# Cache loads issued as two halves, even and odd partitions, from two queues

## The chip, the cores and the metric

The kernel runs on one core of a Trainium2 chip. A core has five engines with instruction streams of their own: TensorE (PE), VectorE (DVE), ScalarE (ACT), GpSimd (POOL) and SyncE (SP). An engine takes its instructions in the order in which the program lists them for it; each may wait for counters (semaphores) that other engines or finished transfers advance. Data moves between the device's memory (HBM) and the on-chip buffer (SBUF, 128 partitions) by DMA. A DMA is issued by an engine as one of its instructions: the issuing engine waits for the semaphores that the transfer needs, hands the transfer to its own queue and goes on; the transfer's end advances another semaphore. SP's queue is called q1 in the profile, ScalarE's q10; the transfers of both run on the core's 16 DMA engines.

The metric is device time in microseconds (us) of one execution; several runs are given by their median. The profile comes from one further execution.

## The reference

Two layers of one decode step for two sequences (B = 2, one token each, width 576). A layer is attention over a cache of 8192 positions with 32 heads of 128, and a gated MLP of width 4608. All is float32, and both layers use the same weights and the same caches.

```python
def _A_ref(x, k_cache, v_cache, wq, wo):
    q = (x @ wq).reshape(B, Sq, H, Dh).transpose(0, 2, 1, 3)
    scores = jnp.einsum("bhqd,bhkd->bhqk", q, k_cache) * (Dh ** -0.5)
    p = _softmax(scores, axis=-1)
    o = jnp.einsum("bhqk,bhkd->bhqd", p, v_cache)
    return o.transpose(0, 2, 1, 3).reshape(B, Sq, H * Dh) @ wo
...
def _B_ref(x, w_gate, w_up, w_down):
    g = jnp.einsum("bsd,df->bsf", x, w_gate)
    u = jnp.einsum("bsd,df->bsf", x, w_up)
    return jnp.einsum("bsf,fd->bsd", _gelu(g) * u, w_down)
...
x = x + _A_ref(_layernorm(x), A_k_cache, A_v_cache, A_wq, A_wo)
x = x + _B_ref(_layernorm(x), B_w_gate, B_w_up, B_w_down)
x = x + _A_ref(_layernorm(x), A_k_cache, A_v_cache, A_wq, A_wo)
x = x + _B_ref(_layernorm(x), B_w_gate, B_w_up, B_w_down)
```

## The kernel before, in words

**Items.** The attention is cut into items: for each sequence 15 pairs of heads (`PAIRS` = 30 items of two heads) and four items of one head (`SINGLE`). The keys or values of a pair are 16384 rows of 128 floats; each partition holds 128 consecutive rows, 64 KB, in 8 parts of 16 rows (`PART`). `Item.source` lays the cache out in this way, partition first. Layer 0 takes the items in rising order, layer 1 in falling order; what layer 0 loads last (the keys of the last two items and the values of the last three, with pieces of others) stays on chip for layer 1 (`KEYS_HELD`, `VALUES_HELD`, `kept`).

**Space.** One tile, `space`, is nearly the whole SBUF: six slots of 32 KB per partition for the caches (a pair takes two), the last of which makes way to four smaller places in a ring for weights and odd pieces. The class `Arena` keeps account of it while the program is written.

**Loads.** `plan_first`, `plan_mlp` and `plan_second` put all loads of weights and caches into one list in the order in which they are wanted. `pump` takes from its head what finds free space, and is called after each `done(key)`, at the point of the program that last reads a piece of data. A load's DMA so stands in the program right behind the reader that frees its place, and waits for that reader's semaphore. All loads are issued by SP, which has nothing else to do. `cache`, `half`, `one` and `several_parts` (whole pairs or items, half items, single parts, several parts) all call `load`, whose DMA is line 168; weights have DMAs of their own (lines 233 to 322), and line 233 (`by_rows`) brings one item's keys by rows. ScalarE issues only the eight small loads of x (line 143) and half of the output (line 1201).

**The attention.** For an item VectorE multiplies the keys by the query (L743, from `multiply`), GpSimd folds the products in half (L772) and VectorE sums them (L775, from `add_up`, which then frees the keys). Maximum and softmax follow: L799, a transposition on PE (L801), L807, PE again (L809), then ScalarE's scaling of the maximum (L824) and its exponentials (L832). PE multiplies the weights by the values (L913, from `values`, which frees them); two of a pair's eight value parts go another way, VectorE L880, GpSimd L883, PE L891 (`weigh`, `folded`). L927, L928, L936 gather an item's context, and L943, L955, L957 divide it. `half_products` (L615) makes layer 1's queries from halves of wq.

At the start of layer 1 the first five items (`waited`) run in units of one part. There ScalarE copies the query to SBUF (L740), GpSimd multiplies the last four rows with it (L759), and ScalarE sums the last seven rows itself (L765):

```python
            if rows < every and k == 0:
                nc.scalar.copy(q, qb[n])
...
            for j in range(r, every):
                nc.scalar.activation(
                    u[:, j, :], u[:, j, :], AF.Copy, accum_out=S[n][:, base(n, k) + j:base(n, k) + j + 1]
                )
```

Near the end of layer 0 ScalarE copies one part of an item's keys to PSUM before VectorE overwrites it with products (L733). The order of the work on each engine is written out by hand in `attention`: in the loop over items the units of item n alternate with softmax, folding, values and context of the items before.

The functions that the diff touches, and those that call them, with the line numbers of the profile:

Of the kernel before, what the change touches and what calls it, by code (L numbers as in the profile page):

```python
# [24 lines left out]
JC = 16  # L25
# [37 lines left out]
ITEMS = [Item(b, h, 2) for h in range(0, H - 2, 2) for b in range(B)]  # L63
# [62 lines left out]
def decode_layers(ctx, tc, x_in, kc, vc, wq, wo, wg, wu, wd, out):  # L126
    nc = tc.nc
# [12 lines left out]
    for c in range(4):  # L140
        for s in range(2):
            lo = 32 * c + s * B
# [16 lines left out]
    def part_at(at, n):  # L159
        return space[:, at:at + n]  # L160
# [4 lines left out]
    def load(at, n, src, lo, hi):  # L165

        t = part_at(at, (hi - lo) * PART).rearrange("p (j d) -> p j d", d=DH)
        nc.sync.dma_start(t, ITEMS[n].source(src)[:, lo * JC:hi * JC, :])

    def cache(key, src, n, slots=None):  # L170

        parts = ITEMS[n].parts

        def make():
            at = arena.pair(key) if slots is None else arena.slots(key, slots, parts)
            if at is None:
                return False
            load(at[0], n, src, 0, parts)
            ready[key] = dict(enumerate(map(part, at)))
            places[key] = at  # L180
            return True

        queue.append(make)

    def half(key, src, n, k, slot):

        def make():
            at = arena.slots(key, (slot,), 4, k)
            if at is None:
                return False  # L190
            load(at[0], n, src, k, k + 4)
            ready.setdefault(key, {}).update((k + i, part(a)) for i, a in enumerate(at))
            return True

        queue.append(make)

    def one(key, src, n, k, where):

        def make():
            at = arena.ring((key, k), PART) if where is None else arena.take((key, k), places[where[0]][where[1]], PART)  # L200
            if at is None:
                return False
            load(at, n, src, k, k + 1)
            ready.setdefault(key, {})[k] = part(at)
            return True

        queue.append(make)
# [250 lines left out]
    for b in range(B):  # L458
        rows = ident.rearrange("p (c v i r) -> p i r v c", c=4, v=4, i=2)[:, :, :, b, :]
# [769 lines left out]
```

## Time and profile before

| | |
|---|---|
| three runs | 2681.36 us median, 2681.06 to 2681.51 |
| the profiled execution | 2681.31 us, of which the span of its instructions is 2679.5 us |
| mean granted TensorE clock | 0.627 |
| read from HBM | 1152.39 MB, 430 GB/s over the span |
| instructions in the span | 15405 |

The page gives the busy time of each engine over the span; PE is the matmuls, PEld the weight loads beside them. L743 is line 743 of the kernel, "x" a count of instructions. A queue's share is the time that its packets took on the 16 DMA engines. In the timeline a row is one instruction or several alike: start, length, engine, line, operation, what it writes and reads; in brackets the idle time of its engine before it and what ended that. SPq and ACTq rows are the sequencers', which issue DMAs; the length there is that of the issue and not of the transfer. The chain of waits follows the last instruction back through what released each step. For the DMA engines the page shows, in 40 slices of the span:

```profile
DMA  9999999999999999999999999999999999999998
GB/s 423 437 429 434 436 434 432 431 436 433 431 434 434 434 433 432 436 428 427 417 417 431 436 433 434 434 430 434 435 432 432 436 434 433 431 437 434 428 430 385
```

### The profile page before, as it was taken

How to read it: one execution, taken by the hardware profiler on the slowest of the kernel's cores; microseconds unless marked ns; L12 is line 12 of the kernel's file. 1: busy time of each engine (PE TensorE's matmuls, PEld its weight loads, DVE VectorE, ACT ScalarE, POOL GpSimd, SP SyncE). 2: the span in 40 equal slices, each digit the busy share in tenths (PEclk: the TensorE clock that was granted, in tenths of full speed). 3: DMA queues.
4: the chain of work that ended last, by engine and by line, in shares of the span. 5: the costliest groups of instructions: out<-in, count | busy, mean ns of one | idle time of the engine just before them, and what ended most of it. 6: DMA issues, size and time to landing. Idle time of an engine off the chain costs nothing.

```text
span 2679.5 us, 15405 instructions
## 1 busy us (share of the span) xinstructions
PE 880.8 (33%) x6198; PEld 268.7 (10%) x6198; DVE 1992.6 (74%) x907; ACT 165.7 (6%) x792; POOL 1560.5 (58%) x411
## 2 busy tenths in 40 slices
PE   1313332232223233334663323223222323332346
PEld 0000000000000000011221000000000000000022
DVE  4877888888788888867038778888888888888740
ACT  0000000000000000001026000000000000000000
POOL 2546676667667666744028457666766666676620
PEclk8666655665665566566986665566566556655678
DMA  9999999999999999999999999999999999999998
GB/s 423 437 429 434 436 434 432 431 436 433 431 434 434 434 433 432 436 428 427 417 417 431 436 433 434 434 430 434 435 432 432 436 434 433 431 437 434 428 430 385
DMA packets 29207, 1153.39 MB, mean 430 GB/s; under 512 B 3256, under 2 KB 3280, under 8 KB 4048
## 3 DMA queue, kind: packets, MB, share of 16 engines
q1 hardware_dynamic: 29096, 1152.40, 99.8%
q8 instruction: 48, 0.79, 0.1%
q14 instruction: 23, 0.19, 0.0%
q10 hardware_dynamic: 40, 0.01, 0.0%
HBM read 1152.39 MB, written 0.00 MB: 430 GB/s over the span
## 4 chain that ended last, share of the span: by engine, by line
DMA 67%; DVE 19%; PE 8%; POOL 2%; ACT 2%; issue 1%; another core or an unknown queue 0%; SPq 0%; POOLq 0%; ACTq 0%; DVEq 0%
DMA space<-in_A_k_cache_dram 59%; DVE space L743 17%; PE acc L891 3%; DMA space<-in_B_w_down_dram 2%; DMA space<-in_B_w_gate_dram 2%; POOL space L772 2%; DVE scores L775 2%; PE bank L658 1%; DMA space<-in_A_v_cache_dram 1%; DMA space<-in_B_w_up_dram 1%; PE bank L809 1%; ACT prz L832 1%; PE acc L913 1%; DMA space<-in_A_wo_dram 1%; PE bank L845 1%
## 5 line engine op out<-in xcount | busy, mean ns | idle before, releaser
L772 POOL TENSOR_TENSOR space<-space 128x3072 f32<-128x3072 f32 (+4 forms) x221 | 1128.4, 5106 | 459.1 <-DVE space L743 330.7
L743 DVE TENSOR_TENSOR space<-space,bank 128x6144 f32<-128x6144 f32 (+4 forms) x223 | 1111.9, 4987 | 344.7 <-DMA space<-in_A_k_cache_dram 273.7
L775 DVE TENSOR_REDUCE scores<-space 128x48 f32<-128x3072 f32 (+4 forms) x223 | 568.7, 2550 | 92.1 <-POOL space L772 92.1
L913 PE MATMUL acc<-space,prz 128*16 128x512 f32 (+1 forms) x3312 | 510.1, 780 | 357.9 <-DMA space<-in_A_v_cache_dram 346.4
L883 POOL TENSOR_TENSOR space<-space 128x2048 f32<-128x2048 f32 x147 | 398.0, 2708 | 392.3 <-DVE space L880 376.8
L658 PE MATMUL bank<-qsb,few 4*64 4x128 f32 (+1 forms) x256 | 46.1, 436 | 894.8 <-DVE space L743 887.1
L880 DVE TENSOR_TENSOR space<-space,bank 128x4096 f32<-128x4096 f32 x49 | 216.6, 4421 | 1.7
L913 PEld LDWEIGHTS acc<-space,prz 128*16 128x16 f32 (+1 forms) x3312 | 108.7, 117 | 742.0 <-issue 449.7
L824 ACT ACTIVATE nbs<-bank 128x2 f32<-128x2 f32 (+1 forms) x68 | 11.6, 171 | 2010.4 <-PE bank L809 1957.1
L658 PEld LDWEIGHTS bank<-qsb,few 4*64 4x64 f32 (+1 forms) x256 | 20.6, 201 | 914.2 <-DVE space L743 897.4
L580 POOL TENSOR_TENSOR rstd<-ve,few 128x1 f32<-128x1 f32 x4 | 2.2, 551 | 171.3 <-DVE ve L578 171.3
L891 PE MATMUL acc<-space,few 128*16 128x512 f32 x98 | 92.6, 1048 | 0.0
L801 PE MATMUL bank<-ident,m 128*1 128x128 f32 x68 | 20.7, 305 | 196.1 <-DVE m L799 195.9
L936 PE MATMUL bank<-few,wide 128*32 128x4 f32 (+1 forms) x272 | 20.9, 200 | 170.1 <-DVE wide L928 170.1
L1153 DVE STREAM_TRANSPOSE gu<-acc 128x288 f32<-128x288 f32 x4 | 1.9, 484 | 92.6 <-ACT acc L1151 92.6
L832 ACT ACTIVATE prz<-scores,nbs 64x128 f32<-64x128 f32 (+1 forms) x128 | 50.7, 396 | 11.7 <-POOL prz L822 8.9
L765 ACT ACTIVATE space<-space 128x128 f32<-128x128 f32 x164 | 48.4, 297 | 19.5 <-DVE space L743 16.5
L809 PE MATMUL bank<-m,few 1*128 1x2 f32 (+1 forms) x136 | 39.0, 353 | 28.1 <-DVE m L807 28.1
L584 DVE TENSOR_TENSOR x<-bank,x 128x144 f32<-128x144 f32 x4 | 1.2, 308 | 59.4 <-PE bank L1186 39.7
L927 DVE TENSOR_TENSOR acc<-acc,few 128x512 f32<-128x512 f32 x34 | 23.5, 691 | 29.2 <-PE acc L913 29.2
L936 PEld LDWEIGHTS bank<-few,wide 128*32 128x32 f32 x272 | 19.1, 154 | 216.0 <-issue 211.0
L955 ACT ACTIVATE oT<-bank,rinv 32x8 f32<-32x8 f32 x108 | 28.1, 260 | 190.1 <-PE bank L936 189.1
(105 smaller groups left out, 495.8 us busy)
## 6 DMA issues: line engine op xcount, KB each, us to landing
space<-in_A_v_cache_dram SPq DMA_DIRECT2D x7, 4096.0 KB
space<-in_A_k_cache_dram SPq DMA_DIRECT2D x6, 4096.0 KB
space<-in_B_w_gate_dram SPq DMA_DIRECT2D x9, 1152.0 KB
space<-in_B_w_up_dram SPq DMA_DIRECT2D x9, 1152.0 KB
space<-in_B_w_down_dram SPq DMA_DIRECT2D x8, 1152.0 KB
space<-in_A_wq_dram SPq DMA_DIRECT2D x9, 1024.0 KB
space<-in_A_wo_dram SPq DMA_DIRECT2D x2, 4608.0 KB
space<-in_A_k_cache_dram SPq DMA_DIRECT2D x4, 2048.0 KB
```

The costliest lines, as they stand in the source:

```text
L658: nc.tensor.matmul(qb[n][to, :], pick[32 * c:32 * c + 4, r:r + 1].to_broadcast([4, P // it.heads]), qsb[32 * c:32 * c + 4, (h % 4) * DH:(h ...
L743: nc.vector.tensor_tensor(out=u[:, :r, :], in0=t[:, :r, :], in1=qb[n].unsqueeze(1).to_broadcast([P, r, DH]), op=ALU.mult)
L765: nc.scalar.activation(u[:, j, :], u[:, j, :], AF.Copy, accum_out=S[n][:, base(n, k) + j:base(n, k) + j + 1])
L772: nc.gpsimd.tensor_tensor(out=half, in0=half, in1=u[:, :r, DH // 2:], op=ALU.add)
L775: nc.vector.tensor_reduce(out=S[n][:, base(n, k):base(n, k) + own_rows(n, k, m)], in_=prod.pop((n, k)), axis=AX.X, op=ALU.add)
L809: nc.tensor.matmul(mT[n][:, :heads], ones[0:1, :], m1[:, :heads], start=True, stop=True)
L832: nc.scalar.activation(pr[at, lo:].rearrange("p (g e) -> p g e", e=4)[:, 0:it.rows // 2 * it.heads:2 * it.heads, :], s[at, :it.rows].rearr ...
L880: nc.vector.tensor_tensor(out=t, in0=t, in1=share.unsqueeze(2).to_broadcast([P, rows, DH]), op=ALU.mult)
L883: nc.gpsimd.tensor_tensor(out=t[:, :rows - less], in0=t[:, :rows - less], in1=t[:, less:rows], op=ALU.add)
L891: nc.tensor.matmul(accumulator(n)[0:16, :], owner[:, 8 * ITEMS[n].b:8 * ITEMS[n].b + 16], part_at(arena.live[key, lo][0], 4 * DH), start=F ...
L913: nc.tensor.matmul(accumulator(n)[32 * c:32 * c + m, :], pr[:, at:at + m], t[g // 4][:, g % 4 * 4:g % 4 * 4 + 4, :].rearrange("p j d -> p ...
L936: nc.tensor.matmul(po[lo:lo + 32, i, :c], t[:, i::GH], of[:, :c], start=True, stop=True)
```

## The change

`load` issues two DMAs where it issued one. The destination and the source are cut by partition: the even partitions are issued by SP, the odd ones by ScalarE. Both halves have the rows of the whole load, 64 KB each for a pair, and 64 partitions. Each half is waited for by whoever reads the data. The point of the program at which they are issued is the same for both: ScalarE's half stands among ScalarE's own instructions there, and waits for the readers that free the place as SP's half does. Loads of weights, the eight loads of x and line 233 stay as they are.

```diff
@@ -165,7 +165,9 @@
     def load(at, n, src, lo, hi):
 
         t = part_at(at, (hi - lo) * PART).rearrange("p (j d) -> p j d", d=DH)
-        nc.sync.dma_start(t, ITEMS[n].source(src)[:, lo * JC:hi * JC, :])
+        rows = ITEMS[n].source(src)[:, lo * JC:hi * JC, :]
+        for engine, p in ((nc.sync, 0), (nc.scalar, 1)):
+            engine.dma_start(t[p::2], rows[p::2])
 
     def cache(key, src, n, slots=None):
```

## The prediction

> **What bounds the kernel now.** First the page: busy time per engine, the queues, the chain that ended last.
>
> ```profile
> PE 880.8 (33%) x6198; PEld 268.7 (10%) x6198; DVE 1992.6 (74%) x907; ACT 165.7 (6%) x792; POOL 1560.5 (58%) x411
> q1 hardware_dynamic: 29096, 1152.40, 99.8%
> DMA 67%; DVE 19%; PE 8%; POOL 2%; ACT 2%; issue 1%; another core or an unknown queue 0%; SPq 0%; POOLq 0%; ACTq 0%; DVEq 0%
> ```
>
> SP's queue (q1) alone keeps the 16 DMA engines 99.8% busy; two thirds of the chain is DMA. What is left to gain by keeping the engines fuller is 0.2% of 2679.5 us, 5.4 us. The view by stretches (the stretch and its length, busy time of PE, its weight loads, DVE, ACT and POOL with their instructions, the granted clock, the busy share of the DMA engines, GB/s) says at what rate they run:
>
> ```profile
> 2.00:26.00 24.00, 0.23 (x1) 0.23 (x2) 4.12 (x24) 0.00 (x0) 0.00 (x0) 1.00 0.97 417
> 26.00:82.00 56.00, 12.94 (x89) 3.51 (x89) 36.03 (x14) 2.90 (x7) 20.57 (x5) 0.64 0.99 431
> 300.00:700.00 400.00, 115.74 (x628) 31.85 (x628) 331.35 (x119) 17.90 (x75) 268.78 (x63) 0.59 1.00 433
> 1180.00:1240.00 60.00, 23.52 (x125) 8.41 (x125) 39.86 (x38) 6.35 (x21) 25.07 (x13) 0.66 1.00 432
> 1283.00:1359.00 76.00, 47.40 (x695) 19.66 (x684) 5.77 (x26) 1.42 (x4) 0.55 (x1) 0.98 1.01 418
> 1388.00:1464.00 76.00, 33.84 (x186) 10.45 (x181) 62.76 (x73) 53.37 (x336) 58.96 (x48) 0.67 1.01 426
> ```
>
> In steady attention it is 433 GB/s with a share of 1.00. One turn of that stage in the timeline:
>
> ```profile
> 568.44 6.55 DVE L743 TENSOR_TENSOR space<-space,bank 128x6144 f32<-128x6144 f32 x1 [3.43 <-DMA space<-in_A_k_cache_dram]
> 576.29 0.17 ACT L824 ACTIVATE nbs<-bank 128x2 f32<-128x2 f32 x1 [29.44 <-PE bank L809]
> 579.98 0.33 SPq L168 DMA_DIRECT2D space<-in_A_k_cache_dram  x1
> 607.14 6.55 DVE L743 TENSOR_TENSOR space<-space,bank 128x6144 f32<-128x6144 f32 x1 [4.70 <-DMA space<-in_A_k_cache_dram]
> ```
>
> DVE waits for keys, and the load issued at 579.98 is used at 607.14, 27.2 us later. Its 8.39 MB (two heads of 8192 x 128 floats) take 19.4 us at 433 GB/s, so some 7.8 us of transfers were still queued ahead. That queue is the cover: an issue may come 7.8 us late in this stage before an engine has nothing to move.
>
> **The change part by part.**
>
> *More and smaller transfers.* Line 168 issues this many loads:
>
> ```profile
> L168 SPq DMA_DIRECT2D space<-in_A_k_cache_dram x72: 327/328/424, 10.8 to 2512.6; - x72
> L168 SPq DMA_DIRECT2D space<-in_A_v_cache_dram x69: 327/328/431, 37.9 to 2545.8; - x69
> ```
>
> 141 more DMAs, the same bytes in the same rows. The nearest row is the stretch 1180 to 1240, whose loads are of 4 MB as most halves will be: 432 GB/s against 433 is 0.02 us for 4.19 MB, at most 141 x 0.02 = 3 us, and within rounding. The far bound is the stretch from 1283 with loads of 1152 KB: 1.18 MB at 418 takes 2.82 us, at 433 2.72, so 0.10 us each, 14 us in all; but its pieces are 9 KB and ours stay 8 to 64 KB. Below nothing is excluded but for the 5.4 us above. I take 1 us.
>
> *The rate with two queues at work.* No row shows half the partitions moving in each of two queues. Nearest is the start, where ScalarE's eight small loads of x run beside the bulk of SP's: 417 GB/s in 2 to 26 against 431 in 26 to 82, at worst 3.3%, with the start itself in it. The cache loads are 1152.4 MB less 101.4 MB of weights (shapes of the inputs, twice) and 2.4 MB of line 233, so 1048.6 MB, 2422 us at 433: the upper bound of this kind is 80 us, the lower 0. I take 0, since a packet of a given size has the same work in either queue and the engines were full.
>
> *Issuing from ScalarE, steady state.* An issue costs its sequencer 0.33 us, and what stands behind a waiting issue waits too. In program order the key load of 579.98 stands behind ScalarE's exponentials, which follow its L824 of 576.29, and ahead of the next L824, one turn (607.14 - 568.44 = 38.7 us) later; a value load stands between the same two. That next L824 needs the next item's maximum, which comes after what the loads wait for. So ScalarE, 6% busy, is there in time and holds nobody: 0 us, covered by an idle of 29.44 us in the row above.
>
> *The start.*
>
> ```profile
> 44.62 6.55 DVE L743 TENSOR_TENSOR space<-space,bank 128x6144 f32<-128x6144 f32 x1 [16.60 <-DMA space<-in_A_k_cache_dram]
> 73.04 0.33 SPq L168 DMA_DIRECT2D space<-in_A_k_cache_dram  x1
> ```
>
> Now wq (9.4 MB) goes first, then the first keys, used at 44.6. After the change the odd half of those keys goes beside wq, behind ScalarE's loads of x, and the odd half of the second keys beside their even half: the first keys are complete up to 4.19 MB later, 9.7 us. The next issue, now at 73.04, moves with it. Queued by then are 9.4 + 3 x 8.39 = 34.6 MB, 80 us at 433, done at about 82: a cover of 9 us. The term is 1 us (0 to 3).
>
> *End of layer 0.*
>
> ```profile
> 1218.78 1.86 ACT L733 COPY kept<-space 128x2048 f32<-128x2048 f32 x1
> 1222.09 2.28 DVE L743 TENSOR_TENSOR space<-space,bank 128x2048 f32<-128x2048 f32 x1
> 1227.54 0.33 SPq L168 DMA_DIRECT2D space<-in_A_v_cache_dram  x1
> 1228.52 2.29 DVE L743 TENSOR_TENSOR space<-space,bank 128x2048 f32<-128x2048 f32 x1 [3.03 <-DMA space<-in_A_k_cache_dram]
> 1269.19 3.60 PE L913 MATMUL acc<-space,prz 128*8 128x512 f32 x16 [1.50 <-DMA space<-in_A_v_cache_dram]
> 1279.58 1.90 PE L913 MATMUL acc<-space,prz 128*8 128x512 f32 x16 [3.10 <-DMA space<-in_A_v_cache_dram]
> ```
>
> The load of 1227.54 takes the slot that PE's values free. In the program it stands ahead of the copy to `kept` (L733), and the in-place product at 1222.09 may not start before that copy. So copy and product move to about 1227.9 and 1229.7, and the next item's product from 1228.52 to about 1233.1: 4.6 us late. PE's waits for data at 1269 and 1279, 1.50 + 3.10, take that up. 1 us (0 to 4).
>
> *Start of layer 1, the main term.* Here ScalarE sums rows itself (L765) and is 70% busy.
>
> ```profile
> 1380.97 0.54 SPq L268 DMA_DIRECT2D space<-in_A_wq_dram  x1
> 1382.31 0.27 ACT L740 COPY qs<-bank 128x128 f32<-128x128 f32 x1 [0.43 <-PE bank L658]
> 1382.61 1.75 DVE L743 TENSOR_TENSOR space<-space,bank 128x1536 f32<-128x1536 f32 x1 [12.26 <-ACT qs L740]
> 1388.40 0.33 SPq L168 DMA_DIRECT2D space<-in_A_k_cache_dram  x1
> 1389.78 1.04 PE L615 MATMUL acc<-space,xt 128*4 128x512 f32 x8 [0.60 <-DMA space<-in_A_wq_dram]
> 1390.84 0.41 ACT L730 COPY space<-prz 128x264 f32<-128x264 f32 x1 [0.98 <-PE acc L615]
> 1405.57 0.33 SPq L168 DMA_DIRECT2D space<-in_A_v_cache_dram  x1
> 1422.28 0.30 ACT L765 ACTIVATE space<-space 128x128 f32<-128x128 f32 x1
> 1424.79 0.33 SPq L168 DMA_DIRECT2D space<-in_A_k_cache_dram  x1
> 1424.61 1.75 DVE L743 TENSOR_TENSOR space<-space,bank 128x1536 f32<-128x1536 f32 x1 [2.06 <-ACT qs L740]
> 1436.19 0.31 ACT L765 ACTIVATE space<-space 128x128 f32<-128x128 f32 x1 [2.48 <-DVE space L743]
> 1438.53 1.75 DVE L743 TENSOR_TENSOR space<-space,bank 128x1536 f32<-128x1536 f32 x1 [1.71 <-ACT qs L740]
> 1439.77 0.33 SPq L168 DMA_DIRECT2D space<-in_A_k_cache_dram  x1
> ```
>
> The load of 1388.40 is recorded inside `half_products(0)`, where PE frees a quarter of wq, ahead of the loop over heads and so ahead of the first L740. On SP it waits alone. On ScalarE the copy L740 stands behind it, and behind that DVE's first product of the layer: both move from 1382.3 to 1388.8, 6.4 us. Of that 0.98 goes into the wait that ScalarE's L730 had for PE anyway; 5.4 us stays. Later two more loads wait where ScalarE works now: 1424.79 stands ahead of sums that began at 1422.28 (2.5 + 0.33 us), 1439.77 ahead of sums from 1436.19 (3.6 + 0.33). Behind both comes an L740 that DVE waits for. Some ten other issues add 0.33 each where ScalarE is busy, say 1 us of it on the path. So DVE is late by 6.4 us near 1421, 9.2 from 1425, 13 from 1440.
>
> The cover: the quarter of wq issued at 1380.97 is used at 1389.78, 8.8 us later, of which its 1.05 MB take 2.5 at 418; 6.3 us were ahead of it. From there to 1405.57 the plan issues 1024 + 2 x 1152 + 1024 + 2048 + 3 x 1024 KB = 9.70 MB, 22.8 us at 426, and 24.6 us go by: 4.5 us are left. To 1439.77 come 3072 + 2 x 2048 + 1024 + 2048 + 4096 KB, 34.5 us of work in 34.2 us: 4.8 us. After that come loads of 4 MB, 29.5 us of work in the 24 to the next turn: 10 us. The DMA engines lack work by the largest of lateness less cover: 6.4 - 4.5 = 2, 9.2 - 4.8 = 4.4, 13 - 10 = 3. With the time from an issue to its first byte, which no row shows apart, I take 5 us (0 with full absorption, 13 without cover). Time the engines stand idle is lost for good, as everything later is bound by them.
>
> **The sum** is made against the profiled execution, 2681.31 us (span 2679.5 and 1.8 around it); the median of the runs, 2681.36, is the same. 2681.3 + 1 + 0 + 0 + 1 + 1 + 5 = **2689 us**, +0.3%. About 0.2% (5.4 us) is what a measurement of this kernel can tell from no change; the line to slower is 2686.7.
>
> **The rivals.**
>
> *Nothing is lost (chance 0.22).* The even halves of SP alone keep the engines fed while ScalarE holds back the odd ones, and the 4.5 to 5 us of cover at the start of layer 1 are enough because DVE makes up its lateness in waits of its own. For it: share 1.01 throughout that stretch. Against it: DVE is 83% busy there (62.76 of 76). It decides if DVE's lateness at 1440 stays under 5 us. 2681.3 + 1 + 1 = 2683.
>
> *The halves move more slowly (0.16).* If 64 partitions are dealt out so that two DMA engines write to the same place while another place has none, a packet takes up to twice as long: 1048.6 MB at 216 instead of 433 is 2422 us more, about 5100; a mix in which one packet in thirty meets another costs the 80 us of the bound above, 2770. Against it: in 1283 to 1359 weights whose source has 64 rows run at 418, not at half. For it: none of these has 64 partitions at its destination. [...]
>
> *Gain (0.06).* Loads that no longer wait in one line fill the idle 0.2%: 2681.3 - 5 = 2676. Against it: the share of 1.00 at 433 in 400 us.
>
> *ScalarE's waits have no cover (0.08).* The lateness of 13 us at layer 1, 4 at the end of layer 0 and 3 at the start are paid in full: 2702.
>
> **How the numbers follow.** My forecast has 0.48; its own range is 2684 to 2697, about a sixth of it under 2686.7. Slower: 0.40 + 0.16 + 0.08 = 0.64; same: 0.08 + 0.22 = 0.30; faster 0.06. The range 2680 to 2760 takes in the forecast, nothing lost, the waits without cover and most of the 80 us bound of the rate; the doubled packets above it (0.12) and the gain (0.06) stay out.
>
> **What would show it.** q10 carries about 524 MB, q1 the rest, and steady stretches stay at 433 GB/s. The first L740 of layer 1 comes 6 us later against the load at its side, DVE's wait for it grows, and the DMA share dips between 1390 and 1445, some 5 us of idle in all. ScalarE's waits in steady state are unchanged. I am wrong if steady stretches run below 430 GB/s, if that dip is missing, or if ScalarE holds DVE in steady state.

## The result and the profile after

| | median, us | runs |
|---|---|---|
| before, beside it | 2681.44 | 2681.06 to 2682.32 |
| changed kernel | 2694.11 | 2693.40 to 2694.61 |

The ratio is 1.0046, with a 95% interval from 1.0034 to 1.0059: slower by 12.7 us. Ratios leave out runs more than 1.5% above the fastest of the same kernel, which only e7 below has (three of six). The profiled execution has a span of 2692.1 us, 12.6 more than before. In the changed kernel the line numbers are higher by 2 (L743 is now L745, L740 is L742, L765 is L767, L168 is L170).

The page, as before: busy time, the 40 slices of GB/s, the two queues, the chain of waits.

```profile
PE 878.6 (33%) x6198; PEld 270.6 (10%) x6198; DVE 1992.7 (74%) x907; ACT 165.3 (6%) x792; POOL 1561.1 (58%) x411
GB/s 405 435 436 432 429 435 432 436 434 432 434 433 432 432 434 433 435 428 427 417 391 401 435 435 432 433 433 435 433 435 433 432 432 434 433 435 432 433 429 382
q1 hardware_dynamic: 20072, 628.11, 54.4%
q10 hardware_dynamic: 11320, 524.31, 45.1%
DMA 66%; DVE 19%; PE 9%; POOL 3%; issue 1%; ACT 1%; ACTq 0%; DVEq 0%; another core or an unknown queue 0%; POOLq 0%; SPq 0%
```

The engines' busy times are those of before within 2.2 us. The bytes are split between two queues, and almost every slice has its old rate. Three slices don't: the first (405, was 423) and the 21st and 22nd (391 and 401, were 417 and 431), which are the start of the program and the start of layer 1. The view by stretches, with the same bounds as before (the last two columns are the busy share of the DMA engines and GB/s), says the same:

```profile
2.00:26.00 24.00, 0.40 (x2) 0.40 (x2) 4.13 (x24) 0.00 (x0) 0.00 (x0) 1.00 0.87 373
26.00:82.00 56.00, 12.51 (x83) 2.65 (x82) 33.70 (x12) 2.12 (x3) 18.44 (x4) 0.66 1.01 431
300.00:700.00 400.00, 116.16 (x628) 31.99 (x628) 330.57 (x118) 17.89 (x75) 269.01 (x64) 0.59 1.00 433
1180.00:1240.00 60.00, 22.67 (x145) 7.33 (x133) 34.34 (x28) 6.88 (x22) 21.94 (x11) 0.70 1.00 431
1388.00:1464.00 76.00, 34.88 (x182) 10.79 (x178) 52.25 (x64) 44.28 (x274) 48.22 (x40) 0.64 0.95 380
```

The loss stands in two rows: 373 for 417 GB/s in the first 26 us, 380 for 426 in 1388 to 1464. Since the same bytes are moved, it can be followed through the span: for each time t of before, take the bytes that the DMA engines had moved, and see how much later another kernel had moved as many. This table is worked out from the packets' records; e1 to e12 are the experiments below.

```
us later than before, when as many bytes had been moved
at us  after   e1    e2    e3    e4    e6    e8    e9    e12
   20   -0.1   0.0   0.0   0.0   0.0   0.0   0.0   0.0   0.0
   30    2.9   3.2   0.0   3.1   0.0   0.0   3.1   0.0   0.0
  100    2.9   3.1   0.2   3.1   2.5   0.0   3.1   0.5   0.0
 1000    3.0   3.2   0.1   3.3   2.7   0.0   3.3   0.8   0.1
 1380    2.7   3.2   0.2   3.0   2.7   0.0   3.0   1.1   0.0
 1400    6.9   3.1   3.8   3.1   6.3   3.1   3.0   1.0   3.1
 1420    9.5   3.0   6.3   3.3   8.9   4.8   3.4   1.1   4.3
 1440   11.0   3.3   7.2   3.3  10.4   5.1   3.3   1.0   4.6
 1460   11.6   3.1   7.8   3.7  11.2   5.7   3.1   1.1   5.5
 1540   12.0   3.0   7.7   4.1  11.9   5.6   3.1   1.2   5.4
 2500   12.1   3.1   7.8   4.2  11.9   5.7   3.4   1.3   5.4
```

The count is of all 16 DMA engines together. In the changed kernel 2.9 us are lost before 30 us, nothing from there to 1380, 9.3 between 1380 and 1540, and 0.1 from there to 2500. The other half microsecond of the 12.6 comes behind the last row.

**The first 3 us.** The timeline (start, length, engine, line) shows when the first cache loads are issued and first used; the last row is of the view of waits: SP's queue at line 170, what it waited for, us in all, times, the longest.

```profile
25.24 5.01 SPq L170 DMA_DIRECT2D space<-in_A_k_cache_dram  x2
25.19 5.10 ACTq L170 DMA_DIRECT2D space<-in_A_k_cache_dram  x2
47.63 6.55 DVE L745 TENSOR_TENSOR space<-space,bank 128x6144 f32<-128x6144 f32 x1 [19.79 <-DMA space<-in_A_k_cache_dram]
SPq L170 <- DMA space<-in_A_wq_dram: 17.3, 1, 17.3
```

Each of the first two rows is two issues: halves of the first keys at 25.2, halves of the second keys near 29.8. Before, SP issued the first keys at 10.80; now both of their halves are held until wq has landed, though wq and the first keys have different columns of `space` (from 31744 up, and below 16384, by the program's constants). By 25 us there is nothing else to move: the stretch 22 to 26 has a DMA share of 0.46, and had 1.08. (The view counts a packet where it starts, so a short stretch can show a little more than 1.)

**The start of layer 1.** These rows answer to those of 1382 to 1440 in the prediction.

```profile
1391.62 0.50 ACTq L170 DMA_DIRECT2D space<-in_A_k_cache_dram  x1
1392.16 0.27 ACT L742 COPY qs<-bank 128x128 f32<-128x128 f32 x1 [7.29 <-PE acc L617]
1392.46 1.75 DVE L745 TENSOR_TENSOR space<-space,bank 128x1536 f32<-128x1536 f32 x1 [19.27 <-ACT qs L742]
1433.49 0.50 ACTq L170 DMA_DIRECT2D space<-in_A_k_cache_dram  x1
1434.04 0.31 ACT L767 ACTIVATE space<-space 128x128 f32<-128x128 f32 x1 [2.87 <-PE acc L915]
1436.37 1.75 DVE L745 TENSOR_TENSOR space<-space,bank 128x1536 f32<-128x1536 f32 x1 [5.03 <-ACT qs L742]
1451.63 0.50 ACTq L170 DMA_DIRECT2D space<-in_A_k_cache_dram  x1
1454.57 1.75 DVE L745 TENSOR_TENSOR space<-space,bank 128x1536 f32<-128x1536 f32 x1 [6.00 <-ACT qs L742]
```

ScalarE's half stands ahead of its copy L742. ScalarE stands idle 7.29 us there, until PE (matmuls L617) has freed the place, issues at 1391.62, copies at 1392.16, and only then can DVE start the layer: at 1392.46, where 1382.61 + 3.0 was due, after a wait of 19.27 us (was 12.26). The two other loads that wait on ScalarE hold DVE in the same way, 5.03 us (was 2.06) and 6.00 (was 1.71).

### The profile page after: what moved, and what is told of

It is laid out like the page before. It is cut to its first block, busy times and chain, and to the rows that moved or that the text cites. A ratio compares the mean times of both kernels' runs of the same rounds, so it can differ in the third digit from the quotient of the medians.

```text
span 2692.1 us, 15866 instructions
## 1 busy us (share of the span) xinstructions
PE 878.6 (33%) x6198; PEld 270.6 (10%) x6198; DVE 1992.7 (74%) x907; ACT 165.3 (6%) x792; POOL 1561.1 (58%) x411
## 4 chain that ended last, share of the span: by engine, by line
DMA 66%; DVE 19%; PE 9%; POOL 3%; issue 1%; ACT 1%; ACTq 0%; DVEq 0%; another core or an unknown queue 0%; POOLq 0%; SPq 0%
DMA space<-in_A_k_cache_dram 57%; DVE space L745 17%; PE acc L893 3%; DMA space<-in_B_w_up_dram 3%; POOL space L774 2%; DVE scores L777 2%; DMA space<-in_A_wo_dram 2%; PE bank L660 1%; PE acc L915 1%; DMA space<-in_A_v_cache_dram 1%; DMA space<-in_A_wq_dram 1%; PE bank L811 1%; DMA space<-in_B_w_down_dram 1%; DMA space<-in_B_w_gate_dram 1%; ACT prz L834 1%
## 5 line engine op out<-in xcount | busy, mean ns | idle before, releaser
L745 DVE TENSOR_TENSOR space<-space,bank 128x6144 f32<-128x6144 f32 (+4 forms) x223 | 1111.9, 4987 | 359.7 <-DMA space<-in_A_k_cache_dram 270.3
L767 ACT ACTIVATE space<-space 128x128 f32<-128x128 f32 x164 | 48.3, 295 | 27.4 <-DVE space L745 13.2
L761 POOL TENSOR_TENSOR space<-space,qs 128x512 f32<-128x512 f32 x23 | 29.4, 1279 | 32.4 <-ACT qs L742 32.4
```

What stands on the lines that cost most here:

```text
L745: nc.vector.tensor_tensor(out=u[:, :r, :], in0=t[:, :r, :], in1=qb[n].unsqueeze(1).to_broadcast([P, r, DH]), op=ALU.mult)
L761: nc.gpsimd.tensor_tensor(out=u[:, rows:every, :], in0=t[:, rows:every, :], in1=q.unsqueeze(1).to_broadcast([P, every - rows, DH]), op=ALU ...
L767: nc.scalar.activation(u[:, j, :], u[:, j, :], AF.Copy, accum_out=S[n][:, base(n, k) + j:base(n, k) + j + 1])
```

## The experiments

The theory: 9 us come from ScalarE's in-order stream at the start of layer 1, 3 us from the first load's wait for wq. The rivals: halves cost something each, two queues cost something, the loss is spread over all issues. A counter of the calls of `load` picks loads: 0 is the first keys, 70 to 83 are the 14 loads issued from 1388 to 1450. Medians are beside those of before in the same group of runs, 2681.70 for e1 to e4, 2681.56 for e5 to e8, 2681.45 for e9 to e12.

### e1: both halves by SP

```diff
-        for engine, p in ((nc.sync, 0), (nc.scalar, 1)):
+        for engine, p in ((nc.sync, 0), (nc.sync, 1)):
```

> Both halves issued by SP, ScalarE issues none. Theory (ScalarE's in-order stream costs 9 us at the start of layer 1, the first load's wait for wq 3 us at the start): the 9 us go, the 3 us stay, 2684.4. Rival 'halves' (141 more DMAs, smaller ones, completion semaphores used again sooner): all 12 us stay, 2693 to 2694. Rival 'two queues' (the sharing of the DMA engines between two queues): both losses go, 2681.4.

2684.86 us, ratio 1.0011 (1.0003 to 1.0020). The 9 us are gone and 3 stay. The stretch at the start of layer 1 is whole again:

```profile
1388.00:1464.00 76.00, 35.94 (x197) 10.41 (x189) 62.83 (x73) 54.61 (x343) 58.62 (x48) 0.70 1.01 427
```

In the table e1 loses 3.2 us before 30 us and nothing after: 141 more DMAs, each of half the size, cost nothing that shows.

### e2 and e3: one part of the change alone

```diff
+        i = len(calls)
+        calls.append(i)
+        if not 70 <= i < 84:        # e3: if 70 <= i < 84:
+            nc.sync.dma_start(t, rows)
+            return
```

> Only the 14 loads at the start of layer 1 are halves by SP and ScalarE, the other 127 are whole on SP. Theory: 2681.4 + 9 = 2690.5, with the same waits of VectorE for ScalarE's copies as in the changed kernel. Rival 'spread out' (the loss is a little for each of 141 issues or DMAs): 12.7 x 14/141 = 1.3, so 2682.7.

> The reverse: those 14 loads are whole on SP, the other 127 are halves by SP and ScalarE. Theory: the 3 us of the start alone, 2684.4. Rival 'spread out': 12.7 x 127/141 = 11.4, so 2692.8.

e2 took 2690.60 us, ratio 1.0033 (1.0020 to 1.0045); e3 2685.87, 1.0014 (1.0005 to 1.0023). The 14 loads at the start of layer 1 bring 8.9 us, the other 127 bring 4.2, and 8.9 + 4.2 is within half a microsecond of the whole, 12.7. A loss spread over the issues would have put 1.3 on the one and 11.4 on the other. e3's column of the table has 3.1 us at the start and 0.8 more between 1440 and 1540, where the halves begin again.

### e8: only the three that wait ahead of ScalarE's copies are whole

```diff
+        if i in (70, 79, 81):
+            nc.sync.dma_start(t, rows)
+            return
```

> The three loads of the start of layer 1 that wait ahead of ScalarE's copies (1388.40, 1424.79 and 1439.77 us) are whole on SP, the other 138 are halves. Theory that these three waits are all of the 9 us: 2684.4, with what the other eleven issues cost by themselves on top (at most 11 x 0.5 us): up to 2686. Rival 'all fourteen share the loss': 9 x 11/14 = 7 stay, 2691.5.

2686.01 us, ratio 1.0016 (1.0008 to 1.0025). With three of 141 loads back on SP, the loss at the start of layer 1 is gone (table: 3.0 at 1380, 3.1 at 1460). The first row is of the timeline, the second of the stretches:

```profile
1385.60 1.75 DVE L751 TENSOR_TENSOR space<-space,bank 128x1536 f32<-128x1536 f32 x1 [12.27 <-ACT qs L748]
1388.00:1464.00 76.00, 34.83 (x196) 10.31 (x188) 62.80 (x73) 54.03 (x343) 58.70 (x48) 0.71 1.01 426
```

DVE's first product waits 12.27 us as before, and comes 3.0 us later than before, which is the loss at the start of the program. The eleven other issues on ScalarE, 0.5 us each, cost nothing there that the table shows. The median is 1.2 us above that of e1, in which ScalarE issues no cache load; the two intervals overlap, so whether ScalarE's other issues cost about a microsecond in all isn't settled.

### e6 and e12: one load alone, halved or whole on ScalarE

```diff
+        if i != 70:                 # e6: load 70 alone is halved
+            nc.sync.dma_start(t, rows)
+            return
...
+        (nc.scalar if i == 70 else nc.sync).dma_start(t, rows)      # e12: no halves
```

> One load alone is halved, the one of 1388.40 us at the start of layer 1, whose odd half stands on ScalarE ahead of the layer's first copy of the query. Theory: VectorE's first product waits about 6 us longer and the DMA engines lack work for all or most of it before 1420: 2681.4 + 4 to 6 = 2685.5 to 2687.5. Rival 'cover as predicted' (4.5 us of 5.4 hidden): 2682 to 2683. Rival 'spread out': 2681.5.

> All loads are whole; one of them, that of 1388.40 us at the start of layer 1, is issued by ScalarE in place of SP. Theory (the wait in ScalarE's in-order stream ahead of its first copy is the cause, not the halving): the loss of the run in which this load alone is halved, 5.7 us, 2687.3. Rival 'the half in SP's queue fed the engines' (without it the loss grows): 2689 or more. Rival 'it is the halving': 2681.6.

e6 took 2687.99 us, ratio 1.0023 (1.0014 to 1.0033); e12 2687.68, 1.0024 (1.0015 to 1.0033). One DMA on another engine costs 6.2 to 6.4 us, halved or not, a little over the 4 to 6 expected of e6. So it is not the halving, and an even half in SP's queue doesn't feed the engines meanwhile. e12 isolates the mechanism, so it is the place to see how a late engine becomes idle DMA engines. Its stretches:

```profile
1386.00:1394.00 8.00, 3.67 (x20) 0.40 (x18) 4.79 (x3) 1.83 (x11) 2.52 (x2) 1.00 1.01 424
1394.00:1396.00 2.00, 0.00 (x0) 0.00 (x0) 2.00 (x3) 1.72 (x12) 1.41 (x1) 0.73 0.66 274
1396.00:1398.00 2.00, 0.00 (x0) 0.00 (x0) 2.00 (x2) 1.63 (x11) 1.21 (x2) 0.50 0.49 116
1398.00:1400.00 2.00, 0.00 (x0) 0.00 (x0) 0.50 (x2) 1.57 (x10) 2.00 (x3) 0.50 0.78 303
1400.00:1408.00 8.00, 4.52 (x21) 1.72 (x25) 5.94 (x7) 3.02 (x19) 3.14 (x3) 0.50 0.97 379
```

and three rows of its timeline:

```profile
1388.47 0.36 ACTq L172 DMA_DIRECT2D space<-in_A_k_cache_dram  x1
1388.87 0.27 ACT L744 COPY qs<-bank 128x128 f32<-128x128 f32 x1 [6.95 <-PE acc L619]
1396.64 0.33 SPq L172 DMA_DIRECT2D space<-in_A_k_cache_dram  x1
```

The copy is 6.6 us late (1388.87 against 1382.31). DVE frees the keys that much later, so SP's next load is issued at 1396.64 instead of 1390.08. By the packets' records 5.4 us of work was queued at 1390.08 in the kernel before; at 1396.64 it is 0.06. The DMA engines run dry near 1395, with 116 GB/s in 1396 to 1398. The first packets of the new load start at 1397.60, 1.0 us after its issue.

### e4, e5 and e9: the start

```diff
+        if i == 0:                  # e5: i == 0 or 70 <= i < 84; e9: i < 3 or 70 <= i < 84
+            nc.sync.dma_start(t, rows)
+            return
```

> Only the first load of keys is whole on SP, all others are halves. Theory: it no longer waits for wq, is issued near 10.8 us instead of 25.2, and 2.9 us go: 2691.2. Rival 'ScalarE's x loads' (the start is late because the odd halves stand behind the loads of x on ScalarE): the second and third loads are still held, so 2693 to 2694.

> The first load and the 14 loads at the start of layer 1 are whole on SP, the other 126 are halves by SP and ScalarE. Theory: nothing is left of the loss, 2681.4, and q10 still carries some 490 MB at 433 GB/s. Rival 'halves or two queues cost a little each': 2683 to 2692.

e4 took 2693.44 us, ratio 1.0042 (1.0029 to 1.0056), e5 2685.21, 1.0013 (1.0004 to 1.0021). Half of the theory held: the whole first load doesn't wait for wq and is issued at 10.62. But the time didn't come back, in either kernel. The number is that of the rival 'ScalarE's x loads', though not its reason: SP and ScalarE issue the second keys at the same moment, 29.84 and 29.85, so the loads of x hold nobody. The table says where it went: 0.0 at 30 us is followed by 2.5 at 100 (e5, not in the table, has 2.4 there and loses nothing more at the start of layer 1). e4's timeline, with the stretch 82 to 100 of e4:

```profile
10.62 0.33 SPq L173 DMA_DIRECT2D space<-in_A_k_cache_dram  x1
29.84 0.57 SPq L176 DMA_DIRECT2D space<-in_A_k_cache_dram  x1
29.85 0.57 ACTq L176 DMA_DIRECT2D space<-in_A_k_cache_dram  x1
54.41 6.55 DVE L751 TENSOR_TENSOR space<-space,bank 128x6144 f32<-128x6144 f32 x1 [26.51 <-DMA space<-in_A_k_cache_dram]
82.84 0.47 SPq L176 DMA_DIRECT2D space<-in_A_k_cache_dram  x1
82.00:100.00 18.00, 9.35 (x67) 2.74 (x71) 17.28 (x6) 1.15 (x5) 9.62 (x2) 0.62 0.97 405
```

and the same stretch before:

```profile
82.00:100.00 18.00, 8.64 (x64) 2.06 (x64) 16.59 (x5) 0.38 (x2) 15.85 (x3) 0.78 1.07 463
```

The first keys, issued at their old time, are complete 9.8 us later (54.41 against 44.62). From 29.85 the odd half of the second keys moves in ScalarE's queue beside the rest of the first keys in SP's queue; before, both whole loads were in SP's queue (issued at 10.80 and 29.95), and in e9 below, where they are again, the first product starts at 44.74. The next issue moves from 73.04 to 82.84, behind the end of what is queued, and the DMA engines lose 2.5 us.

> The first three cache loads and the 14 at the start of layer 1 are whole on SP, the other 124 are halves. Theory 'ahead of the first keys' (where only the first load is whole, the odd halves of the second and third load run in ScalarE's queue beside it, delay the first keys by 10 us and empty the DMA engines for 2.5 us after 82 us): with three whole loads the first product is back near 44.6 us, the fourth load is issued near 73 us, and the time is that of before, 2681.6. Rival 'a loss of the halves in general': 2685, as with the first load alone whole.

With the first three loads whole the first rows of before are back:

```profile
44.74 6.55 DVE L751 TENSOR_TENSOR space<-space,bank 128x6144 f32<-128x6144 f32 x1 [16.61 <-DMA space<-in_A_k_cache_dram]
73.16 0.57 SPq L176 DMA_DIRECT2D space<-in_A_k_cache_dram  x1
```

e9 took 2683.50 us, ratio 1.0007 (0.9998 to 1.0015): no difference from before that the interval excludes, with 124 of 141 loads in halves from two queues. Its profiled span is 1.5 us above that of before, and the table shows 1.3 of it: 0.5 by 100 us, 0.8 by 1000, 1.1 by 1380. Whether that is a cost of the halves, of the second queue or of this execution isn't settled.

### e7, e10 and e11: which 64 partitions

```diff
-        for engine, p in ((nc.sync, 0), (nc.scalar, 1)):
-            engine.dma_start(t[p::2], rows[p::2])
+        for engine, p in ((nc.sync, 0), (nc.scalar, P // 2)):               # e7
+            engine.dma_start(t[p:p + P // 2], rows[p:p + P // 2])
...
+            engine.dma_start(t[p::2], rows[p * P // 2:(p + 1) * P // 2])     # e10
...
+            engine.dma_start(t[p * P // 2:(p + 1) * P // 2], rows[p::2])     # e11
```

> The halves are partitions 0 to 63 by SP and 64 to 127 by ScalarE, in all 141 loads. [...] Rival 'wait for wq whatever the shape of the half': 2694.

> Even partitions by SP and odd ones by ScalarE, as in the changed kernel, but the even ones are filled from the first 64 rows of the source, the odd ones from the last 64, so that the rows land in other partitions and the result is not the reference's; the work is the same. Theory 'places in SBUF' (the blocks 0 to 63 and 64 to 127 are slow as targets): 433 GB/s and about 2694. Rival 'places in HBM' (each half then reads one head's 4 MB alone): about 216 GB/s and 5064.

> The reverse: partitions 0 to 63 are filled from the even rows of the source by SP, 64 to 127 from the odd rows by ScalarE; the rows land in other partitions and the result is not the reference's. Theory 'places in SBUF': about 216 GB/s in the attention and 5064. Rival 'places in HBM': 433 GB/s and about 2691.

In six runs e7 took 4999.95 to 5092.69 us, median 5064.33; the ratio is 1.8745 (1.8668 to 1.8822). e10 took 2693.11 and e11 5023.52, one run each. The stretch 300 to 700, of e7:

```profile
300.00:700.00 400.00, 57.57 (x321) 16.34 (x321) 159.79 (x58) 8.89 (x37) 125.56 (x28) 0.54 1.00 215
```

of e10:

```profile
300.00:700.00 400.00, 117.46 (x628) 32.28 (x628) 330.19 (x118) 17.87 (x75) 268.82 (x64) 0.59 1.00 433
```

and of e11:

```profile
300.00:700.00 400.00, 60.13 (x341) 17.03 (x345) 154.90 (x55) 8.88 (x37) 121.83 (x27) 0.55 1.00 213
```

The same bytes in the same rows move at half the rate where a DMA's target is a block of 64 neighbouring partitions, with its rows from a block of the source (e7, 215 GB/s) or every second one (e11, 213), and at the full rate where it is every second partition (433 in e10 and in the changed kernel). The DMA engines show a share of 1.00 in both: the share counts packets under way, so it doesn't tell a slow packet from a full engine. GB/s does: a packet of 64 KB takes 4.87 us in e7 and 2.42 in e10, in either queue.

Two queues, one for each block, don't make up for it. By e7's packet records those of the two queues start in alternating groups of about 16, and on average 12.3 of the 16 packets under way in 300 to 700 us belong to the same queue (11.8 in e10, where it does no harm), so most of the engines are on one block at a time. Whether that is why the two blocks don't add up isn't shown.

So the 433 GB/s and the 2691 us that the author expected of e7 were wrong; that blocks don't wait for wq, also expected, held. The first cache issues of SP in e7:

```profile
13.88 22.43 SPq L170 DMA_DIRECT2D space<-in_A_k_cache_dram  x2
```

in e10:

```profile
25.39 5.01 SPq L170 DMA_DIRECT2D space<-in_A_k_cache_dram  x2
```

and in e11:

```profile
13.71 21.86 SPq L170 DMA_DIRECT2D space<-in_A_k_cache_dram  x2
```

Only the halves whose target is every second partition wait. This is a dependence in the program and no need of the data; how it comes about stays open.

## Why the prediction was right, and where it was not

The forecast was 2689 us with a range of its own of 2684 to 2697; 2694.11 lies in it. The largest term had the right mechanism and about half of the measured size. Term by term, against the profiled execution:

| term | predicted | shown |
|---|---|---|
| more and smaller transfers | +1 | 0 (e1, flat from 30 us on) |
| rate with two queues | 0 | 0 (433 GB/s) |
| issuing from ScalarE, steady state | 0 | 0 (table flat from 1540 on) |
| start | +1 (0 to 3) | +2.9 |
| end of layer 0 | +1 (0 to 4) | 0 |
| start of layer 1 | +5 (0 to 13) | +9.3 |

The terms shown add up to 12.2 of the 12.6 us of span.

**The rate.** Whether half the partitions move at the full rate was the open point behind the rival of slower halves. They do if they are every second one (433 GB/s in 300 to 700 us), and the rival fell; the same edit with two blocks gives 5064 us (e7), near the rival's upper end of 5100. That two DMA engines write to the same place, as the rival supposed, no run shows; shown is a packet of 64 KB that takes 4.87 us into blocks and 2.42 into every second partition (e10).

**The start.** The size came out at the upper end of its bounds, for a reason the prediction didn't have: the strided halves wait for wq. That it lies within the bounds is luck. The mechanism that it did have, first keys up to 9.7 us late against a cover of 9, is real. It shows as soon as that wait is taken away (e4: 9.8 us late, 2.5 lost). In the changed kernel the wait hides it, because both halves of the first keys then start together, ahead of the second keys. So removing the first cause alone gains nothing.

**The end of layer 0.** The mechanism is there and costs nothing. In the changed kernel the copy to `kept` stands behind ScalarE's issue:

```profile
1230.29 0.50 ACTq L170 DMA_DIRECT2D space<-in_A_v_cache_dram  x1
1230.83 1.87 ACT L735 COPY kept<-space 128x2048 f32<-128x2048 f32 x1 [8.20 <-PE bank L938]
1232.73 2.29 DVE L745 TENSOR_TENSOR space<-space,bank 128x2048 f32<-128x2048 f32 x1 [6.80 <-ACT kept L735]
1282.53 1.90 PE L915 MATMUL acc<-space,prz 128*8 128x512 f32 x16 [0.87 <-DMA space<-in_A_v_cache_dram]
```

Less the 3.0 us of the start, the copy is at 1227.8 and the product at 1229.7, the two times that were predicted. Of PE's waits for value data downstream, 1.50 and 3.10 us, 0.87 is left (last row): they took the lateness up, and the table has 3.0 at 1000 and 2.7 at 1380.

**The start of layer 1.** The lateness was right, and so were the three loads that cause it. The first copy comes 6.9 us later against before (1392.16 - 1382.31 - 3.0, predicted 6.4), and SP's issue behind the third wait moves from 1444.22 to 1460.37, 13.2 us after taking off 3.0 (predicted 13). The step that failed is the cover, "4.5 us are left" and "4.8 us". It was worked out from the quarter of wq issued at 1380.97 and used 8.8 us later: 2.5 for its bytes, so "6.3 us were ahead of it". Counting the bytes issued and not yet landed in the trace of before gives less:

```
issue     queued ahead, us   all bytes up to the load's last had moved at
1380.97   3.9                1387.58
1390.08   5.4                1400.58
1405.57   2.4                1415.71
1439.77   3.3                1453.32
```

The two differ because the parts of a load don't land together. The semaphore of the load of 1380.97 was advanced 16 times, 15 times between 1387.10 and 1388.48 and the last time at 1389.74; PE used the load at 1389.78. So 6.3 us goes by the part that landed last, and 3.9 by all bytes together.

A queue of that length isn't all cover either: in e12 the issue at 1396.64 found it empty, and the rate was back only after 1398, which makes about 1.5 us, an estimate from this one dip. At 1390.08, the first issue that DVE's lateness reaches and one where the prediction gave no cover, 5.4 - 1.5 = 3.9 us are left for 6.6: 2.7 lost, and the table has 3.1 at 1400 for e12. The issue of 1405.57 comes 5.0 us late in e12 (1410.52), with 2.4 - 1.5 = 0.9 left: 4.1 lost by then, and e12 shows 4.3 at 1420. In the changed kernel SP's issue of 1439.77 comes 8.9 us late (1451.63, less 3.0), with 3.3 - 1.5 = 1.8 left: 7.1, where the prediction had 9.2 - 4.8 = 4.4. So the cover accounts for 2.7 of the 4.9 us between that 4.4 and the measured 9.3. The rest stays open: the changed kernel had lost 8.3 by 1440 and 9.3 by 1540, and e12 5.5 by 1460, one to two us more than this count gives. That the third wait brings the last of it in the changed kernel fits its 6.00 us on DVE, but no run took that wait alone.

**The rivals.** *Nothing is lost* was to be decided by DVE's lateness at 1440 staying under 5 us; it was 8.9 (SP's issue of 1439.77 came at 1451.63, less 3.0). *Waits without cover* priced the start of layer 1 at 13; 9.3 lies nearer to it than to the 5 of the forecast. *Gain*: no stretch runs faster than before.

## What to carry to other kernels

A DMA that an engine with other work issues can hold that engine for as long as the transfer's place is taken, and with it everything behind it in program order: here ScalarE stood idle 7.29 us, and DVE's first product of the layer came 6.9 us late. Look not at the 0.5 us of the issue but at what stands behind the issues that wait: here three of 141 made the whole loss at the start of layer 1. Take the cover from the bytes in the queue at the issue, less the time from an issue to its first bytes (1.0 us in e12), and not from the time between an issue and the use of its data, which goes by the part that lands last (in the load of 1380.97 it was 1.26 us after the others). And if a load is cut in two by partitions, try every second partition before blocks: here these ran at 433 GB/s, blocks of 64 at 215.

## What the runs showed that was not expected

The first load in halves waits for wq, which lies in other columns, where its target is every second partition (issued at 25.2 us, against 10.6 whole and 13.9 in blocks). Two losses at the same place hid each other: 2.9 us from that wait, and 2.5 from the second queue's halves running beside the first keys, of which a kernel shows one or the other. And the second queue undid the order in which loads are wanted: an odd half issued 19 us after the first keys delayed them by 9.8.
